# A banded attention and a gated feed-forward in one program: where the first weights stand in the load queue, and what the search for the order charges

## The chip, the cores and the metric

The kernel runs on one core of one Trainium2 chip. The metric is the device time of an execution in microseconds (us), median of three runs. A core has four engines that matter here, each with a queue of its own that is worked off in order: PE (matrix multiply into PSUM; its weight loads are shown apart as PEld), DVE (vector), ACT (scalar and activation), POOL. SP only starts transfers (DMA); they too start in the order of its queue.

## The reference

Attention for 4 batches, 8 heads, 768 positions, head size 64, in which a query sees the keys less than 96 positions behind it and the first 8 keys; a bias of -slope times distance is added ahead of the softmax. The heads of a position side by side are a row of 512 numbers, and each of the 3072 rows goes through a gated feed-forward (called "moe" in the code):

```
x = attention(q, k, v)              # [3072, 512]
out = ((x @ w_a) * (x @ w_b)) @ w_out   # w_a, w_b [512, 1536], w_out [1536, 512]
```

The inputs are float64 and reach the chip as pairs of 32-bit words.

## The kernel before

The 3072 rows are cut into 24 blocks of 128, and these into 8 units of 4, 2, 3, 3, 3, 3, 3 and 3 blocks (`UNITS`). For a unit the attention gives `x`; the feed-forward then runs over `NF` = 12 chunks `f` of 128 hidden columns. The attention of unit u+1 is worked in beside the feed-forward of unit u, so only the first unit's attention has no matrix work to hide behind.

**Attention of the first unit** (`first`, `quad`). It goes by four pairs of heads, c = 0 to 3, each in two halves j. For a half: scores `ps` on PE (line 789), the maximum on DVE (617), exp on ACT (633), sum and reciprocal on DVE (648, 655), normalizing on DVE, POOL or ACT (667, 665), transposes `pt` on PE (692), copies `pf` to SBUF (419), and the product with the values into `pa` on PE (742). After both halves of pair c, `pa` is written as two parts, `xh` (rounded for PE, line 419) and the rest `xl` (DVE, 849); for pair 3 the names of both tiles are `xl0` and `xl0_3`. The second unit is done in the same way with one half for a pair (`ps..1_c_0`). Inputs of pair c are `raw0_c` (queries and keys) and `v0_c`, loaded by `fetch_first` through SP (line 544). Pair 0's `raw0` is loaded and scaled ahead of that.

**Weights** (`load_w`). Chunk f comes in two pieces, g = 0 and 1, of 768 KB: `wr{f}_{g}` (line 455). Piece 0 holds the chunk of `w_a` and half of that of `w_b`, piece 1 the rest and `w_out`. Each is turned from float64 into a rounded and a rest part, `wt{f}_{g}`, by seven or eight steps of 768 columns: ACT 461 (absolute value of the high word) and 498 (low word); DVE 468, 478 (clip, shift), 488, 507 (join); the cast to the rounded part on ACT (419) or DVE (421); the rest on DVE (429). This is done once, beside the first unit, and the pieces stay.

**Feed-forward** (`moe`). For a chunk, `p0` and `p1` (line 990) take 12 matmuls each, three for each pair c: xh by the rounded weight, xl by it, xh by the rest. ACT copies `p0`, DVE multiplies by `p1` (1029), the result is split into `hh` and `hl` (419 or 421, 429), and line 1008 adds the product with `w_out` to the accumulators `acc`.

**What sets the order.** Every step is given to a planner (`Schedule.op`) with a due time `due` in ns, the engines that may do it and a cost on each. `Schedule.order` hands out the steps: an engine that is free takes, of the steps whose inputs are there, the one due first. What it writes is the order of each engine's queue; on the chip each step then waits for its inputs only. `Schedule.search` looks for better due times for all steps due ahead of `t2`, which is the end of the second unit's feed-forward: it shifts a share of the due times by random amounts and keeps a trial that ends earlier.

```
START = 52000
WLEAD = 6000
TRIES = 400
SHARE = 0.03
SPREAD = 4000.0
...
        loads = [self.fetch_first(c, -1e6 + 2 * c) for c in range(NCC)]
...
        for f in range(NF):
            self.load_w(f, t + f * steps[0] - WLEAD)
```

So in this plan the inputs of all four pairs are due ahead of everything, and the loads of chunk 0 are due at 46000 with their other steps; SP, which takes what is due first, starts the weights right after the seven inputs.

Of the kernel before, what the change touches and what calls it, by code (L numbers as in the profile page):

```python
# [27 lines left out]
NCC = DM // P  # L28
# [15 lines left out]
OLD = ()  # L44

START = 52000
WLEAD = 6000
LOADLEAD = 8000
SPLITLEAD = 3000
# [6 lines left out]
SWAP = 640.0  # L56
PRICE = {"dve": 2.0, "pool": 2.0}


TRIES = 400  # L60
SHARE = 0.03
SPREAD = 4000.0
TRACE = False
LAGS = {"pe": 200.0, "act": 270.0, "dve": 230.0, "pool": 290.0, "dma": 2300.0}
BIG = float(2**38)
# [149 lines left out]
class Schedule:  # L215
# [22 lines left out]
    def search(self, limit, tries, share, spread):  # L238


        rnd = random.Random(1)
        ops = [op for op in self.ops if op.due < limit]
        dues = {op.index: op.due for op in ops}
        best = self.order(ops, dues)[1]
        for _ in range(tries):
            trial = dict(dues)
            for op in ops:
                if rnd.random() < share:
                    trial[op.index] += rnd.gauss(0.0, spread)
            end = self.order(ops, trial)[1]  # L250
            if end < best:
                best, dues = end, trial
        return self.order(self.ops, {op.index: dues.get(op.index, op.due) for op in self.ops})

    def order(self, ops, dues):
        for op in ops:
            op.fresh(dues[op.index], dues)
        for op in ops:
            for buf in op.bufs:
                buf.left += 1  # L260
        free = {e: 0.0 for e in self.SYNC}
        ready = {e: [] for e in self.SYNC}
        heap = []
        head = {t: 0 for t in self.tags}
        live = {t: 0 for t in self.tags}
        taken = set()
        out = []
        now = 0.0
        port = 0.0

        def arrive(op):
            for e in op.costs:
                insort(ready[e], (op.at, op.index, op))

        def fits(op):
            for b in op.bufs:
                if b in taken:
                    continue
                queue = self.tags[b.tag]
                if head[b.tag] >= len(queue) or queue[head[b.tag]] is not b or live[b.tag] >= b.bufs:  # L280
                    return False
            return True

        def wins(op, e):
            if len(op.costs) == 1:
                return True
            at = {}
            for o, c in op.costs.items():
                at[o] = max(free[o], now) + c * PRICE.get(o, 1.0)
                for due, index, other in ready[o]:  # L290
                    if (due, index) >= (op.at, op.index):
                        break
                    if len(other.costs) == 1 and fits(other):
                        at[o] += BACKLOG * other.costs[o]
            return at[e] <= min(at.values()) + 40.0

        for op in ops:
            if not op.before:
                arrive(op)
        while len(out) < len(ops):  # L300
            started = True
            while started:
                started = False
                for e in free:
                    if free[e] > now:
                        continue
                    for item in ready[e]:
                        op = item[2]
                        if e in op.port and port > now:
                            continue  # L310
                        if fits(op) and wins(op, e):
                            break
                    else:
                        continue
                    for o in op.costs:
                        ready[o].remove(item)
                    for b in op.bufs:
                        if b not in taken:
                            taken.add(b)
                            head[b.tag] += 1  # L320
                            live[b.tag] += 1
                    op.engine = e
                    op.t0 = now
                    out.append(op)
                    free[e] = now + op.costs[e]
                    if e in op.port:
                        port = free[e]
                    heappush(heap, (free[e], 0, op.index, op))
                    started = True
            if not heap:  # L330
                raise RuntimeError("no order")
            now, kind, _, op = heappop(heap)
            if kind == 0:
                for nxt in op.after:
                    if nxt.index not in dues:
                        continue
                    if op.engine == "pe" and tuple(nxt.costs) == ("pe",):
                        lag = 0.0
                    else:
                        lag = (op.lag or self.SYNC[op.engine]) + nxt.spare  # L340
                    nxt.ready = max(nxt.ready, now + lag)
                    nxt.before -= 1
                    if not nxt.before:
                        heappush(heap, (nxt.ready, 1, nxt.index, nxt))
                heappush(heap, (now + (op.lag or self.SYNC[op.engine]), 2, op.index, op))
            elif kind == 1:
                arrive(op)
            else:
                for b in op.bufs:
                    b.left -= 1  # L350
                    if not b.left:
                        live[b.tag] -= 1
        return out, now


def act(n, psum=False):
# [18 lines left out]
class Fast:  # L375
# [61 lines left out]
    def load_w(self, f, due):  # L437
# [3 lines left out]
        for g in range(2):  # L441
# [9 lines left out]
            mi = lambda m0=m0: self.wm[:, m0 : m0 + WN]  # L451
            m = lambda mi=mi: mi().bitcast(F32)
            op(
                due,
                lambda e, f=f, g=g, raw=raw: nc.sync.dma_start(raw[:, :].bitcast(I64), self.wts[f, g]),
                writes=[(raw, "lo"), (raw, "hi")],
                dma=2184,
# [364 lines left out]
    def first(self, end):  # L822


        sp = self.sbuf
        six = [sp([P, 3 * WIDE], F32R, k, k + "0") for k in ("xh", "xl")]
        two = [sp([P, 512], F32R, "o", f"xl0_{c}", 2) for c in (2, 3)]
        xh = [(six[0], 0), (six[0], WIDE), (six[0], 2 * WIDE), (six[1], 0)]
        xl = [(six[1], WIDE), (six[1], 2 * WIDE), (two[0], 0), (two[1], 0)]
        homes = {  # L830
            "q": ("hl", WIDE),
            "s": (("psS", "acc0"), ("p0", "acc2")),
            "pt": ("psT", "p1", "acc1"),
            "t": (("kk", MAXK), ("raw", MAXC)),
            "pf": (("hh", WIDE), ("v", 2 * MAXV * D)),
        }
        loads = [self.fetch_first(c, -1e6 + 2 * c) for c in range(NCC)]
        step = end / NCC
        for c in range(NCC):
            pa = self.bank("psA", f"pa0_{c}")  # L840
            for j in range(2):
                self.quad(0, c, j, c * step + (j + 1) * step / 2, *loads[c], pa, homes)
            (hi, h0), (lo, l0) = xh[c], xl[c]
            get = lambda b, b0=0: lambda: b[:, b0 : b0 + WIDE]
            due = (c + 1) * step
            self.copy(due, get(hi, h0), get(pa), WIDE, [pa], [(hi, c)], psum=True)
            self.plan.op(
                due,
                lambda e, lo=get(lo, l0), hi=get(hi, h0), pa=get(pa): self.nc.vector.tensor_sub(
                    lo(), pa(), hi()  # L850
                ),
                [pa, (hi, c)],
                [(lo, -c - 1)],
                dve=dve(WIDE),
            )
        return xh, xl
# [211 lines left out]
    def run(self):  # L1068
        self.open()
        t = START  # L1070
        x = self.first(t - 3000)
        steps = []
        for u, pl in enumerate(PLANS):
            nxt = PLANS[u + 1].nb if u + 1 < len(PLANS) else 0
            steps.append(24 * pe(pl.nb * P) + pl.nb * 3 * pe(512) + nxt * H * 700 / NF)
        xs = {0: x}

        def ahead(u, t):
            xs[u] = self.attention(u, t, t + (NF - SLACK) * steps[u - 1])

        for f in range(NF):
            self.load_w(f, t + f * steps[0] - WLEAD)
        t2 = t + NF * (steps[0] + steps[1])
        for u in range(len(UNITS)):
            self.moe(u, t, steps[u], xs[u])
            if u + 1 < len(UNITS):
                ahead(u + 1, t)
            t += NF * steps[u]
        order, end = self.plan.search(t2, TRIES, SHARE, SPREAD)
        if TRACE:  # L1090
            print('MODEL', end)
        with self.tc.manual_schedule():
            for op in order:
                op.emit(op.engine)
# [371 lines left out]
```

## Time and profile before

| | |
|---|---|
| time, median of 3 runs | 741.05 us (739.51 to 741.62) |
| profiled execution | 739.72 us, of which its span of instructions 737.9 us |
| busy share of the span | PE 97%, PEld 87%, DVE 65%, ACT 47%, POOL 1% |
| granted PE clock, mean | 0.994 |
| chain that ended last, by engine | PE 92%, DVE 4%, ACT 2%, DMA 1% |
| transfers | 74.58 MB, mean 101 GB/s, over 300 GB/s in the first tenth of the span |

A row of the profile names line, engine, operation and tiles (output<-input) with shapes, `x` the count, then the time; a bracket gives the idle time of the engine just before and what ended it. A row of stretches gives, for each engine, busy us and in parentheses the count of instructions; then the clock that PE was granted (1.00 is full), the share of the transfer engines, and GB/s. PE's busy time has its clock in it: at half clock the same matmul is busy for twice as long.

### The profile page before, as it was taken

How to read it: one execution, taken by the hardware profiler on the slowest of the kernel's cores; microseconds unless marked ns; L12 is line 12 of the kernel's file. 1: busy time of each engine (PE TensorE's matmuls, PEld its weight loads, DVE VectorE, ACT ScalarE, POOL GpSimd, SP SyncE). 2: the span in 40 equal slices, each digit the busy share in tenths (PEclk: the TensorE clock that was granted, in tenths of full speed). 3: DMA queues.
4: the chain of work that ended last, by engine and by line, in shares of the span. 5: the costliest groups of instructions: out<-in, count | busy, mean ns of one | idle time of the engine just before them, and what ended most of it. 6: DMA issues, size and time to landing. Idle time of an engine off the chain costs nothing.

```text
span 737.9 us, 12581 instructions
## 1 busy us (share of the span) xinstructions
PE 715.4 (97%) x4344; PEld 640.1 (87%) x4344; DVE 480.0 (65%) x1574; ACT 348.8 (47%) x891; POOL 8.9 (1%) x28
## 2 busy tenths in 40 slices
PE   5789999999999999999999999999999999999996
PEld 4567877889988999999999999999999999899996
DVE  5999999958956776287744878268672876321111
ACT  6999967556335353254424544154432544331112
POOL 1000000000000000000000000000000000000000
PEclk9999999999999999999999999999999999999999
DMA  7898211123533234124231443214341242110001
GB/s 282 345 339 326 82 32 33 35 85 110 142 106 113 84 98 116 44 83 110 74 116 44 108 122 96 73 61 107 88 128 55 81 127 62 47 44 0 1 1 47
DMA packets 38520, 74.58 MB, mean 101 GB/s; under 512 B 8496, under 2 KB 21040, under 8 KB 38448
## 3 DMA queue, kind: packets, MB, share of 16 engines
q1 hardware_dynamic: 29232, 65.03, 27.6%
q10 hardware_dynamic: 9216, 8.66, 4.6%
q8 instruction: 36, 0.59, 0.3%
q14 instruction: 36, 0.29, 0.1%
HBM read 50.07 MB, written 6.29 MB: 76 GB/s over the span
## 4 chain that ended last, share of the span: by engine, by line
PE 92%; DVE 4%; ACT 2%; DMA 1%; issue 0%; DVEq 0%; ACTq 0%; SPq 0%
PE p L990 54%; PE acc L1008 27%; PE pa L742 5%; PE ps L915 4%; PE ps L789 2%; DVE t L617 1%; PE pt L692 1%; DMA v<-qkv 0%; DMA nv<-ns 0%; DMA raw<-qkv 0%; DVE kk L429 0%; DVE t L667 0%; ACT kk L419 0%; ACT xh L419 0%; ACT wr L498 0%
## 5 line engine op out<-in xcount | busy, mean ns | idle before, releaser
L990 PE MATMUL p<-xh,wt 128*128 128x384 f32 (+2 forms) x1488 | 418.3, 338 | 1.1 <-DVE wt L429 0.6
L990 PEld LDWEIGHTS p<-xh,wt 128*128 128x128 f32 x1488 | 270.3, 188 | 15.3 <-issue 3.4
L990 PE MATMUL p<-xl,wt 128*128 128x384 f32 (+2 forms) x816 | 270.1, 341 | 0.3 <-DVE xl L429 0.3
L1008 PE MATMUL acc<-wt,hh 128*128 128x512 f32 x576 | 202.5, 394 | 0.0
L990 PEld LDWEIGHTS p<-xl,wt 128*128 128x128 f32 x816 | 153.9, 189 | 10.1 <-issue 1.0
L1008 PEld LDWEIGHTS acc<-wt,hh 128*128 128x128 f32 x576 | 108.2, 188 | 20.5 <-issue 1.3
L1029 DVE TENSOR_TENSOR raw<-p,raw 128x384 f32<-128x384 f32 (+2 forms) x96 | 52.9, 551 | 96.6 <-PE p L990 93.1
L1008 PE MATMUL acc<-wt,hl 128*128 128x512 f32 x288 | 113.1, 393 | 0.0
L633 ACT ACTIVATE t<-t,sm 128x232 f32<-128x232 f32 (+2 forms) x120 | 56.5, 472 | 93.9 <-DMA pf<-wm 77.6
L419 ACT COPY raw<-p 128x384 f32<-128x384 f32 (+2 forms) x84 | 39.9, 475 | 104.1 <-PE p L990 101.5
L1008 PEld LDWEIGHTS acc<-wt,hl 128*128 128x128 f32 x288 | 54.2, 188 | 7.6
L429 DVE TENSOR_TENSOR hl<-raw,hh 128x384 fp32r<-128x384 f32 (+2 forms) x95 | 52.1, 548 | 12.7 <-ACT hh L419 12.0
L617 DVE CUSTOM_DVE_ANT_0 t<-ps,rel 128x232 f32<-128x232 f32 (+1 forms) x100 | 38.1, 397 | 25.6 <-PE ps L915 23.2
L419 ACT CAST hh<-raw 128x384 fp32r<-128x384 f32 (+2 forms) x69 | 35.5, 515 | 39.2 <-DVE raw L1029 33.0
L742 PEld LDWEIGHTS pa<-pf,v 128*64 128x64 f32 x640 | 35.5, 138 | 13.0 <-issue 7.4
L742 PE MATMUL pa<-pf,v 128*64 128x128 f32 x640 | 43.7, 280 | 2.9 <-ACT pf L419 1.3
L633 ACT ACTIVATE wm<-wm,sm 128x232 f32<-128x232 f32 (+2 forms) x72 | 34.0, 472 | 23.8 <-DVE sm L617 20.1
L429 DVE TENSOR_TENSOR kk<-raw,kk 64x348 fp32r<-64x348 f32 (+1 forms) x90 | 41.6, 463 | 2.8
L915 PE MATMUL ps<-kk,ql 128*128 128x232 f32 (+2 forms) x144 | 39.4, 275 | 0.0
L915 PE MATMUL ps<-kk,qh 128*128 128x232 f32 (+2 forms) x144 | 38.5, 270 | 0.5 <-DVE sm L617 0.4
L665 ACT ACTIVATE wm<-wm,sm 128x232 f32<-128x232 f32 (+2 forms) x58 | 27.5, 478 | 23.3 <-DVE sm L655 21.0
L709 DVE STREAM_TRANSPOSE wm<-wm 128x256 f32<-128x256 f32 (+1 forms) x72 | 29.6, 414 | 6.7 <-ACT wm L665 5.7
(87 smaller groups left out, 666.8 us busy)
## 6 DMA issues: line engine op xcount, KB each, us to landing
wr<-wts SPq DMA_DIRECT2D x24, 768.0 KB, 10.8
raw<-qkv SPq DMA_DIRECT2D x24, 366.0 KB, 3.1
raw<-qkv SPq DMA_DIRECT2D x24, 314.0 KB, 2.9
v<-qkv SPq DMA_DIRECT2D x16, 384.0 KB, 3.1
out<-o SPq DMA_DIRECT2D x23, 256.0 KB, 2.1
pf<-wm SPq DMA_DIRECT2D x96, 48.0 KB, 2.0
pf<-wm ACTq DMA_DIRECT2D x96, 48.0 KB, 2.0
v<-qkv SPq DMA_DIRECT2D x16, 256.0 KB, 2.7
```

The source lines that it names most:

```text
L419: self.nc.scalar.copy(out(), src())
L429: lambda e: self.engine(e).tensor_sub(out(), a(), b()),
L617: lambda e, j=j, o=o, w=w, neg=neg: nc.vector.tensor_tensor_reduce(t[:, o : o + w], ps[:, o : o + w], neg[:, :w], -(2.0 ** -(h + 1)), 3.0e ...
L633: lambda e, j=j, o=o, w=w: nc.scalar.activation(t[:, o : o + w], t[:, o : o + w], AF.Exp, bias=sm[:, j : j + 1], scale=-1.0, accum_out=sm[ ...
L665: nc.scalar.mul(t[:, o : o + w], t[:, o : o + w], r)
L709: nc.vector.transpose(dst, src)
L742: nc.tensor.matmul(pa[D * s : D * s + D, i * P : i * P + P], v[:, v0 : v0 + D], probs[s, i][1](c), start=c == 0, stop=c == len(slots) - 1,)
L789: nc.tensor.matmul(ps[s][:, o : o + w], qs[r, q0 + m * P : q0 + m * P + P], raw[r, kc : kc + w], start=True, stop=True,)
L915: nc.tensor.matmul(ps[:, :w], q[:, i * P : i * P + P], kk[:, k0 : k0 + w], start=m == 0, stop=m == 1,)
L990: nc.tensor.matmul(p[:, :T], wt(), b[:, b0 : b0 + T], start=c == 0 and n == 0, stop=c == NCC - 1 and n == 2,)
L1008: nc.tensor.matmul(acc[i][:, :], hs[:, i * P : i * P + P], wt(), start=f == 0 and n == 0, stop=f == NF - 1 and n == 2,)
L1029: lambda e, asb=asb, pb=pb: nc.vector.tensor_mul(asb[:, :T], pb[:, :T], asb[:, :T]),
```

## The change

Three things. The load of chunk 0's weights (not its other steps) gets a due time of its own, so that piece 0 is due between the inputs of pair 0 and pair 1, and piece 1 between those of pair 1 and pair 2; the inputs' own due times are spread to make room. The search counts, beside the end of the plan, a charge for waits of PE: for each step on PE the part of the wait ahead of it that exceeds 1300 ns is counted twice, up to 1300 ns a wait. And it makes 1200 trials instead of 400, each shifting 1% of the due times (3% before) by a spread of 8000 ns (4000 before).

```diff
+EARLY = -60000
+LOAD = 4000
...
+IDLE = 1300.0
+FINE = 2.0
...
-TRIES = 400
-SHARE = 0.03
-SPREAD = 4000.0
+TRIES = 1200
+SHARE = 0.01
+SPREAD = 8000.0
...
-        best = self.order(ops, dues)[1]
+        best = self.order(ops, dues)[1:]
...
-            end = self.order(ops, trial)[1]
-            if end < best:
-                best, dues = end, trial
+            found = self.order(ops, trial)[1:]
+            if sum(found) < sum(best):
+                best, dues = found, trial
...
+                    if e == "pe":
+                        fine += min(max(now - free[e] - IDLE, 0.0) * FINE, IDLE)
...
-                due,
+                EARLY + (2 * g + 1) * LOAD if f == 0 else due,
                 lambda e, f=f, g=g, raw=raw: nc.sync.dma_start(raw[:, :].bitcast(I64), self.wts[f, g]),
...
-        loads = [self.fetch_first(c, -1e6 + 2 * c) for c in range(NCC)]
+        loads = [self.fetch_first(c, EARLY + 2 * c * LOAD) for c in range(NCC)]
```

Nearly every row of PE, DVE and ACT up to the end of the second unit changes its place. Three places are shown. Line numbers are 9 higher in the changed kernel; `wr0_1` is chunk 0, piece 1; `raw0_2` and `v0_2` are pair 2 of the first unit; the number at the end of a name is only a count.

The queue of SP from the first load of the plan, before and then now:

```order
L544 DMA v0_0_149<-qkv 128x768
L544 DMA raw0_1_160<-qkv 128x1232
L544 DMA v0_1_178<-qkv 128x768
L544 DMA raw0_2_187<-qkv 128x1232
L544 DMA v0_2_219<-qkv 128x768
L544 DMA raw0_3_237<-qkv 128x1232
L544 DMA v0_3_267<-qkv 128x768
L455 DMA wr0_0_284<-wts 128x768
L455 DMA wr0_1_323<-wts 128x768
L455 DMA wr1_0_355<-wts 128x768
```

```order
L553 DMA v0_0_149<-qkv 128x768
L464 DMA wr0_0_160<-wts 128x768
L553 DMA raw0_1_181<-qkv 128x1232
L553 DMA v0_1_197<-qkv 128x768
L464 DMA wr0_1_211<-wts 128x768
L553 DMA raw0_2_245<-qkv 128x1232
L553 DMA v0_2_271<-qkv 128x768
L553 DMA raw0_3_287<-qkv 128x1232
L553 DMA v0_3_310<-qkv 128x768
L464 DMA wr1_0_326<-wts 128x768
```

Piece 0 moved ahead of six inputs, piece 1 ahead of four; what follows from chunk 1 on stands as it did.

The queue of ACT where it begins the second pair of heads (`t0_0_1_0` is the first half of pair 1), before and then now:

```order
L419 COPY pf1_0_0_0_211<-pt1_0_0_0_200 128x384
L665 ACTIVATE t1_0_0_1_175<-t1_0_0_1_175,sm1_0_0_1_176 128x232
L665 ACTIVATE t0_0_0_1_169<-t0_0_0_1_169,sm0_0_0_1_170 128x232
L633 ACTIVATE t0_0_1_0_234,sm0_0_1_0_235<-t0_0_1_0_234,sm0_0_1_0_235 128x128
L633 ACTIVATE t1_0_1_0_239,sm1_0_1_0_240<-t1_0_1_0_239,sm1_0_1_0_240 128x128
L633 ACTIVATE t0_0_1_0_234,sm0_0_1_0_235<-t0_0_1_0_234,sm0_0_1_0_235 128x256
L419 COPY pf0_0_0_1_265<-pt0_0_0_1_244 128x512
```

```order
L428 COPY pf1_0_0_0_209<-pt1_0_0_0_199 128x384
L470 ACTIVATE wm_219<-wr0_0_160 128x768
L674 ACTIVATE t1_0_0_1_173<-t1_0_0_1_173,sm1_0_0_1_174 128x232
L781 ACTIVATE qs0_1_1_233<-raw0_1_181,sc_79 128x256
L428 COPY pf0_0_0_1_242<-pt0_0_0_1_213 128x512
L507 ACTIVATE wr0_0_160<-wr0_0_160 128x768
L642 ACTIVATE t0_0_1_0_253,sm0_0_1_0_254<-t0_0_1_0_253,sm0_0_1_0_254 128x128
```

Both ACT steps of chunk 0's first piece (470, 507) now stand ahead of the second pair's exp; before, the first of them stood 19 rows further down, behind the second pair's exps.

The queue of PE at the end of the first unit's attention: `pa0_3` is the last product with the values, `ps0_1_0_0` the scores of the second unit's first pair, `p00_0` and `p10_0` chunk 0 (the rows with `xl0`, `xl0_3` are its last pair), `p00_1` chunk 1. Before and then now:

```order
L742 MATMUL pa0_3_564<-pf1_0_3_1_608,v0_3_267 64x128
L789 MATMUL ps0_1_0_0_644<-raw1_0_550,qs1_0_0_638 128x232
L789 MATMUL ps1_1_0_0_646<-raw1_0_550,qs1_0_0_638 128x232
...
L990 MATMUL p00_0_540<-xl0_332,wt0_0_525 128x512
L990 MATMUL p00_0_540<-xl0_3_640,wt0_0_525 128x512
...
L990 MATMUL p00_1_671<-xh0_321,wt1_0_635 128x512
```

```order
L751 MATMUL pa0_3_573<-pf1_0_3_1_603,v0_3_310 64x128
L999 MATMUL p10_0_596<-xh0_297,wt0_1_519 128x512
L999 MATMUL p10_0_596<-xl0_2_557,wt0_1_519 128x512
...
L798 MATMUL ps0_1_0_0_635<-raw1_0_569,qs1_0_0_630 128x232
L798 MATMUL ps1_1_0_0_637<-raw1_0_569,qs1_0_0_630 128x232
...
L999 MATMUL p00_0_483<-xl0_308,wt0_0_417 128x512
L999 MATMUL p00_0_483<-xl0_3_646,wt0_0_417 128x512
...
L999 MATMUL p00_1_665<-xh0_297,wt1_0_628 128x512
```

Three matmuls of chunk 0's third pair now stand between the last product with the values and the scores; `qs1_0_0`, on which the scores wait, was ACT's (row 75 of its queue, behind the last `xh` and a cast) and is now a DVE step ahead of the last `xl`.

More of the change, by code (lines that the diff above doesn't have):

```diff
@@ L269, in order @@
         port = 0.0
+        fine = 0.0
         def arrive(op):
@@ L352, in order @@
                         live[b.tag] -= 1
-        return out, now
+        return out, now, fine
 def act(n, psum=False):
@@ L1088, in run @@
             t += NF * steps[u]
-        order, end = self.plan.search(t2, TRIES, SHARE, SPREAD)
+        order, end, _ = self.plan.search(t2, TRIES, SHARE, SPREAD)
         if TRACE:
```

## The prediction

> **What bounds the kernel now.** I read the page first, then the busy time by stretches, then the timeline at the largest hole.
>
> ```profile
> span 737.9 us, 12581 instructions
> 12.30:24.00 11.70, 11.32 (x100) 8.34 (x97) 8.92 (x51) 10.44 (x36) 0.00 (x0) 0.85 1.02 418
> 24.00:43.30 19.30, 15.85 (x131) 11.17 (x128) 18.76 (x64) 19.30 (x50) 0.74 (x2) 1.00 0.83 320
> 43.30:46.30 3.00, 0.05 (x3) 0.03 (x2) 3.00 (x5) 3.00 (x6) 0.00 (x0) 1.00 0.74 227
> 49.80:60.00 10.20, 10.20 (x45) 8.04 (x44) 9.40 (x19) 10.20 (x20) 0.00 (x0) 1.00 0.99 401
> 60.00:97.00 37.00, 37.00 (x194) 29.24 (x192) 36.72 (x70) 33.43 (x57) 0.00 (x0) 1.00 0.41 157
> 97.00:145.00 48.00, 48.00 (x244) 37.86 (x243) 47.41 (x89) 31.54 (x62) 2.01 (x2) 1.00 0.10 26
> 160.00:205.00 45.00, 44.71 (x353) 41.32 (x354) 40.53 (x177) 23.98 (x81) 0.71 (x1) 1.00 0.45 128
> 205.00:230.00 25.00, 23.81 (x169) 21.22 (x166) 16.62 (x64) 13.76 (x37) 2.02 (x2) 1.00 0.39 112
> 230.00:700.00 470.00, 469.26 (x2850) 434.93 (x2849) 276.88 (x966) 181.83 (x499) 1.42 (x2) 1.00 0.28 80
> ```
>
> Columns: stretch, length, then busy us of PE, PEld, DVE, ACT and POOL, PE's clock, the transfers. From 49.8 us to the end PE hardly stops (470 us with 0.74 idle between 230 and 700). The edit removes no matrix work, so it can only win where PE stands or runs slowly: before 50 us, and in the 1.48 us of idle between 160 and 230 (0.29 + 1.19). Before 43 us PE waits because ACT (19.30 of 19.30) and DVE (18.76) are full. Both had time to spare earlier: 1.26 us of ACT and 2.78 of DVE between 12.3 and 24. The hole itself:
>
> ```profile
> 41.12 1.06 ACT L419 COPY pf<-pt 128x512 f32<-128x512 f32 x2
> 41.75 1.57 PE L742 MATMUL pa<-pf,v 128*64 128x128 f32 x16
> 42.06 1.77 ACT L498 ACTIVATE wr<-wr 128x768 int32<-128x768 uint32 x2
> 43.69 0.91 ACT L461 ACTIVATE wm<-wr 128x768 f32<-128x768 f32 x1
> 44.48 0.59 ACT L419 CAST xl<-pa 128x512 fp32r<-128x512 f32 x1
> 45.37 0.68 DVE L849 TENSOR_TENSOR xl<-pa,xl 128x512 fp32r<-128x512 f32 x1
> 45.67 0.54 ACT L772 ACTIVATE qs<-raw,sc 128x256 f32<-128x256 f32 x1
> 46.27 1.79 PE L789 MATMUL ps<-raw,qs 64*128 64x232 f32 x8 [2.95 <-ACT qs L772]
> 48.05 7.42 PE p L990 x27
> 80.39 3.50 PE p L990 x15
> L461 ACT ACTIVATE wm<-wr 128x768 f32<-128x768 f32 x8 | 7.3, 916 | 0.0
> L498 ACT ACTIVATE wr<-wr 128x768 int32<-128x768 uint32 x12 | 10.7, 925 | 0.0
> ```
>
> The last product with the values ends at 43.32. ACT has three weight steps to do before it writes the last `xh` at 44.48; DVE then writes the last `xl`, ready at 46.05; and PE, at the head of its queue, waits 2.95 us for `qs`, computes scores, and starts chunk 0's last pair only at 48.05, though the inputs were there 2 us earlier. The three rows below the hole give prices: 3.50 us for 15 matmuls at full clock, 0.233 each, and the two weight steps of ACT.
>
> **PE's clock there.** By stretches of 3.41 us:
>
> ```profile
> 8.90:12.31 3.41, 1.48 (x12) 0.98 (x13) 3.41 (x22) 3.21 (x13) 0.00 (x0) 1.00 1.01 401
> 12.31:15.72 3.41, 3.41 (x25) 2.43 (x22) 2.54 (x15) 2.38 (x9) 0.00 (x0) 0.50 1.01 407
> 29.37:32.79 3.42, 2.15 (x18) 1.35 (x13) 3.42 (x19) 3.42 (x12) 0.37 (x1) 1.00 0.98 402
> 43.03:46.44 3.41, 0.46 (x6) 0.22 (x5) 3.41 (x6) 3.41 (x6) 0.00 (x0) 1.00 0.79 255
> 46.44:49.85 3.41, 3.41 (x12) 2.39 (x13) 2.60 (x6) 2.39 (x4) 0.00 (x0) 0.50 1.01 360
> ```
>
> Each of the two stretches at half clock follows one with little work (1.48 and 0.46 us busy); after one with 2.15 the clock stayed. So a hole costs its length and up to 1.7 us (half of 3.41) behind it. The Trainium skill, "TensorE: Matmul & The Clock Gate", Part 1, says that the clock halves after an idle window of some 3.4 us, and that the windows run free. Taken literally (an idle window) this would not have dropped the clock at 12.31, so the trace is stricter than the page; by the page the new hole below is harmless, by the trace it is so only under about 1.3 us (3.42 - 2.15); the sum is the same by both.
>
> **The change, part by part.**
>
> *The loads.*
>
> ```profile
> 5.80 0.33 SPq L544 DMA_DIRECT2D v<-qkv  x1
> 6.18 0.43 SPq L544 DMA_DIRECT2D raw<-qkv  x1
> 9.05 10.62 SPq L455 DMA_DIRECT2D wr<-wts  x9
> 11.43 0.35 DVE L774 TENSOR_SCALAR qs<-raw,sc 128x256 f32<-128x256 f32 x1
> wr<-wts SPq DMA_DIRECT2D x24, 768.0 KB, 10.8
> ```
>
> No transfer is added; two of 0.79 MB move ahead. At the 401 GB/s of the row from 8.90 that is 2.0 us each. Pair 1's input then lands 2.0 us later, pairs 2 and 3 3.9 us later, piece 0 six places earlier. Counting from 7.5 us (0.39 + 0.79 + 0.63 MB), `raw0_1` is there at about 12.0. DVE reaches its first step on it (11.43 before) behind four more short softmax steps, at about 12.3: bounds of the wait 0 and, if the queued transfers share the engines instead of following each other, 3 us. I take 0. The later pairs are needed after 19 us and land before that.
>
> *ACT and DVE up to the last `xl`.* Adding the steps of each queue by their durations, DVE has 0.06 us more to do up to that point than before, ACT 0.27 up to the last `xh` (one more weight cast and a `qs` instead of a low-word step and a copy). What can come earlier is only the spare time: the two weight steps of ACT (0.92 us each) and four of DVE now stand in it. ACT can win 1.26 - 0.27 = 1.0 us at most, and nothing if pair 1's later scores (they stand behind pair 0's first product with the values) open new waits as long. I take 0.5: last `xh` at 44.0, `xl` ready at 45.5.
>
> *PE at the hole.* The last product with the values ends at about 42.8 (ACT's three weight steps again stand between). Then three matmuls of chunk 0 (3 x 0.233 = 0.70), and the scores, 0.9 us at full clock, as `qs` is DVE's and stands 1.35 us of steps ahead of `xl`. They fill the hole to 44.6; 0.9 us remain, which keep the clock. Chunk 0's last pair starts at 45.5 instead of 48.05: **-2.55 us** (-3.05 to -2.05 by the bounds above). From 48.05 to 49.85 PE ran at half clock: **-0.9 us** more. Lead at 50 us: 3.45 us.
>
> *What DVE takes back.* PE may keep the lead only where the weights are ready.
>
> ```profile
> 95.34 0.95 DVE L429 TENSOR_TENSOR wt<-wm,wt 128x768 fp32r<-128x768 f32 x1
> 97.00 0.39 PE L990 MATMUL p<-xh,wt 128*128 128x512 f32 x1
> 101.89 0.95 DVE L429 TENSOR_TENSOR wt<-wm,wt 128x768 fp32r<-128x768 f32 x1
> 107.69 0.63 PE L990 MATMUL p<-xh,wt 128*128 128x512 f32 x2
> L419 ACT CAST wt<-wm 128x768 fp32r<-128x768 f32 x3 | 2.5, 841 | 0.0
> L421 DVE CAST wt<-wm 128x768 fp32r<-128x768 f32 x3 | 1.7, 555 | 0.0
> ```
>
> Chunk 6 is the narrow place: its first piece is ready at 96.29, and PE uses the rest part with its third matmul at 97.46, 1.2 us later. DVE was idle for 0.80 + 0.28 us from 49.8 to 97, and 0.75 in the 46.44 row. The new queue has 1.15 us more of DVE steps ahead of this point (two casts that were ACT's, a product that stood behind). So a lead of 1.2 + 0.5 + 1.83 - 1.15 = 2.4 us at most can pass, and 0.6 if DVE recovers none of its idle time. As PE runs ahead, the products that DVE waits for come earlier too, so most is recovered, and I take 2.1, near the upper end: **+1.35 us**. For chunk 7 the same step ends at 102.84 and is used at 107.69, 4.9 us later; DVE's further 1.3 us of moved casts fit into that.
>
> *The second unit.* The next unit's scores now come closer together at its start, where DVE has room (97 to 145: 47.41 of 48, but from 160 on 40.53 of 45). This may close part of the 1.48 us of idle, or, with the swap transfers between, lose as much; the row of before does not show it. Bounds -1.48 and +1.5, I take **-0.3**.
>
> Sum: -2.55 - 0.9 + 1.35 - 0.3 = -2.4, so 737.3 us against this execution's own 739.72 (737.9 of span, 1.8 around it). It was 1.33 us quicker than the median of the runs, 741.05. The changed kernel's starts will differ from run to run too, as holes before 16 us remain; I add half, 0.6, for its median: **737.9 us**.
>
> **Rivals.** Faster or slower means by over 0.3% of 741.05 (2.2 us), about what runs of this kernel can tell apart: below 738.8, above 743.3.
>
> - *DVE takes the whole lead back.* It is full from 24 to 145 us in either order, and the search does not shorten its work. Then only the 0.6 of the bound above and the second unit's -0.3 remain: 739.72 - 0.9 + 0.6 = 739.4, no change. For: 36.72 of 37.00. Against: 1.83 us of idle time between 46 and 97.
> - *The early weights hold up pair 1* (the other side). SP's queue gives 0.79 MB ahead of `raw0_1`; if the transfers share the engines, DVE stands in order at `qs`, with the weight steps behind it, for 3 us, and at pair 2 for about as long again. A stand of 3.5 us cancels the lead; 6 us make the hole at 43 us longer and bring the half clock back: 739.7 + 2.5 + 0.9 = 743.1, with the run's offset 743.7. For: 10.8 us median from issue to landing, much of it behind others. Against: `raw` landed before 11.43, ahead of all that was queued behind it.
> - *The clock drops again.* If ACT comes 0.5 us later than I take it, the hole passes 1.3 us; half clock takes up to 1.7 back: 739.6. For: the fixed order of three ACT weight steps ahead of the last `xh`.
> - *All comes through*: DVE gives back 0.6 us only and the second unit closes 1.2 us of its idle time: 739.72 - 2.85 - 1.2 + 0.6 = 736.3, or 735.3 with ACT's full 1.0.
> - *Nothing happens*: excluded; the queues differ from the first rows on.
>
> **Chances.** Forecast 0.48, between 736.8 and 738.9; whole lead taken back 0.22; clock again 0.08; all through 0.14; pair 1 held up 0.08. Of the forecast nearly all, and all of the fourth rival, are below 738.8: faster 0.58, within 0.3% 0.34, slower 0.08. The range leaves out the worst of the held-up case and the best of the fourth: 735.3 to 740.8.
>
> **What would show it.**
>
> ```profile
> 23.66 0.89 ACT L461 ACTIVATE wm<-wr 128x768 f32<-128x768 f32 x1
> ```
>
> In the trace after: ACT's first weight step near 13 us instead of 23.66; no wait of PE over 1.3 us between 16 and 50, and full clock from 45 to 50; the first matmul with the last `xl` near 45.5; chunk 6 starting 2 us earlier than 97.00, with short waits of PE for `wt` ahead of it; the unit of 256 columns with less than 1.5 us of idle. I am wrong if DVE stands long at the first `qs` of pair 1, if PE waits repeatedly for `wt` or `hl` between 55 and 97, or if the second unit's swap transfers leave PE idle by more than 3 us.

## The result, and the profile after

The changed kernel takes 735.66 us (median of 6 runs, 735.14 to 737.54) against 741.51 for the kernel before (6 runs): a ratio of 0.9930, 95% interval 0.9914 to 0.9946. The profiled execution took 735.88 us, of which 734.0 are span. The forecast was 737.9, with 735.3 to 740.8 as its range: the direction and the mechanism at the hole held, but the gain is 5.9 us where 3.2 were forecast, and 2.4 us of it come from a term that the sum had at 0.3. The measured time lies 0.4 us above the lower end of the range.

The stretches of the prediction, from the trace of the changed kernel (columns as there):

```profile
core 0 of [0], span 734.0 us
...
12.30:24.00 11.70, 9.97 (x79) 6.89 (x80) 9.74 (x44) 10.81 (x31) 0.37 (x1) 1.00 1.02 419
24.00:43.30 19.30, 16.77 (x152) 12.13 (x148) 18.81 (x73) 19.30 (x57) 0.74 (x1) 1.00 0.77 299
43.30:46.30 3.00, 2.79 (x14) 1.74 (x15) 3.00 (x6) 3.00 (x5) 0.00 (x0) 1.00 0.97 343
49.80:60.00 10.20, 10.20 (x46) 8.22 (x45) 10.00 (x23) 10.20 (x21) 0.00 (x0) 1.00 1.01 418
60.00:97.00 37.00, 37.00 (x197) 28.96 (x196) 36.82 (x70) 31.47 (x54) 0.00 (x0) 1.00 0.42 158
97.00:145.00 48.00, 48.00 (x241) 38.16 (x240) 47.51 (x93) 30.08 (x59) 1.76 (x2) 1.00 0.10 26
160.00:205.00 45.00, 44.69 (x355) 41.16 (x354) 40.60 (x176) 23.81 (x80) 3.00 (x4) 1.00 0.46 131
205.00:230.00 25.00, 24.32 (x163) 22.68 (x162) 14.57 (x47) 9.04 (x23) 0.00 (x0) 1.00 0.32 94
230.00:700.00 470.00, 468.89 (x2850) 434.68 (x2849) 279.05 (x980) 183.40 (x505) 1.42 (x2) 1.00 0.28 80
```

The hole is gone: PE works 2.79 of the 3.00 us from 43.3 on (0.05 before). DVE is as full as it was from 24 to 145 us, and ACT in the rows up to 60 us; behind that ACT has a little less to do (31.47 us of 37 where it had 33.43). From 205 to 230 PE idles 0.68 us instead of 1.19. The timeline at the former hole, with ACT's first weight step ahead of it:

```profile
12.94 0.91 ACT L470 ACTIVATE wm<-wr 128x768 f32<-128x768 f32 x1
...
44.11 1.05 PE L798 MATMUL ps<-raw,qs 64*128 64x232 f32 x8
44.38 0.63 ACT L428 CAST xl<-pa 128x512 fp32r<-128x512 f32 x1
...
44.85 2.55 ACT L507 ACTIVATE wr<-wr 128x768 int32<-128x768 uint32 x3
45.06 0.68 DVE L858 TENSOR_TENSOR xl<-pa,xl 128x512 fp32r<-128x512 f32 x1
...
45.80 1.43 PE L999 MATMUL p<-xl,wt 128*128 128x512 f32 x5 [0.21 <-DVE xl L858]
...
47.27 0.60 ACT L428 COPY raw<-p 128x512 f32<-128x512 f32 x1
...
47.92 0.50 PE L999 MATMUL p<-xh,wt 128*128 128x512 f32 x1 [0.69 <-ACT raw L428]
```

The first matmul with the last `xl` starts at 45.80 instead of 48.05, the scores take 1.05 us instead of 1.79, and the clock is full. Then comes a wait that the prediction did not have: ACT does three weight steps in a row (44.85 to 47.40) before it copies chunk 0's `p`, and PE stands for 0.69 us.

To say where time was won I use the *lead*: every form of matmul counts with its median interval in the trace of before, and the lead of another trace is how much earlier it has done the same sum of matmul work. It is a derived figure; two pairs of rows bear it out, from the timeline and from the group of line 990 (999 after), whose second time is the start of the last such matmul. Before:

```profile
154.46 0.28 PE L990 MATMUL p<-xh,wt 128*128 128x256 f32 x1
```

```profile
L990 PE MATMUL p<-xh,wt x1488: 276/335/504, 34.3 to 727.5; 128*128 128x384 f32 x144, 128*128 128x256 f32 x24, 128*128 128x512 f32 x18
```

After:

```profile
152.06 0.28 PE L999 MATMUL p<-xh,wt 128*128 128x256 f32 x1
```

```profile
L999 PE MATMUL p<-xh,wt x1488: 276/335/504, 31.8 to 723.4; 128*128 128x384 f32 x144, 128*128 128x256 f32 x24, 128*128 128x512 f32 x18
```

The second unit's feed-forward starts 2.4 us earlier, the last `p` 4.1 us. In between the lead is 2.4 us at 60 us, 2.4 still at 145, 4.8 at 250, and 4.1 at the end. So there are two gains, one at the hole and one in 190 to 245 us, and a small loss behind.

### The profile page after: what moved, and what is told of

Same layout as the page of the kernel before. It is cut to its first block, busy times and chain, and to the rows that moved or that the text cites. A ratio compares the mean times of both kernels' runs of the same rounds, so it can differ in the third digit from the quotient of the medians.

```text
span 734.0 us, 12602 instructions
## 1 busy us (share of the span) xinstructions
PE 713.0 (97%) x4344; PEld 638.9 (87%) x4344; DVE 482.6 (66%) x1583; ACT 343.4 (47%) x881; POOL 9.3 (1%) x29
## 4 chain that ended last, share of the span: by engine, by line
PE 85%; DVE 5%; ACT 3%; DMA 3%; issue 1%; ACTq 1%; SPq 0%; DVEq 0%
PE p L999 50%; PE acc L1017 25%; PE pa L751 5%; PE ps L924 4%; DMA pf<-wm 2%; ACT t L642 1%; PE ps L798 1%; DVE wm L718 1%; PE pt L701 1%; ACTq L732 1%; DVE t L626 1%; ACT t L674 1%; DMA nv<-ns 0%; ACT wm L642 0%; DMA raw<-qkv 0%
## 5 line engine op out<-in xcount | busy, mean ns | idle before, releaser
L924 PE MATMUL ps<-kk,ql 128*128 128x128 f32 (+1 forms) x144 | 39.5, 275 | 0.0
L924 PE MATMUL ps<-kk,qh 128*128 128x128 f32 (+1 forms) x144 | 38.3, 268 | 0.0
L657 DVE TENSOR_SCALAR sm<-sm 128x1 f32<-128x1 f32 (+1 forms) x168 | 24.0, 146 | 16.9 <-ACT t L642 13.2
```

The costliest lines, as they stand in the source:

```text
L657: lambda e: nc.vector.tensor_scalar_add(sm[:, 2 * n : 3 * n], sm[:, n : 2 * n], 1e-9),
L924: nc.tensor.matmul(ps[:, :w], q[:, i * P : i * P + P], kk[:, k0 : k0 + w], start=m == 0, stop=m == 1,)
```

## The experiments

All twelve runs. Lead is that of the profiled execution of each over the trace of before shown above, at 60 us, at 250 us and at the last `p`. Ratios, with 95% intervals, are over all runs against those of the kernel before on the same chip (medians 741.77 to 741.98 there); they need not be the quotients of the two medians. The trace of before is some 2 us shorter than these medians, so a gain in the median comes out larger than a lead at the end.

| run | median us | ratio | profiled us | lead 60 / 250 / end |
|---|---|---|---|---|
| before again | 741.94 | 1.0002 (0.9993 to 1.0012) | 741.69 | -1.2 / -2.0 / -1.7 |
| after again | 735.49 | 0.9918 (0.9905 to 0.9930) | 735.27 | 2.7 / 5.3 / 4.3 |
| loads only | 737.11 | 0.9942 (0.9927 to 0.9957) | 738.03 | 2.4 / 2.0 / 1.7 |
| search only | 737.16 | 0.9946 (0.9930 to 0.9962) | 735.99 | 1.3 / 3.2 / 4.0 |
| no charge | 735.99 | 0.9925 (0.9911 to 0.9939) | 734.63 | 2.1 / 4.3 / 5.2 |
| charge, old tries | 740.99 | 0.9992 (0.9977 to 1.0007) | 739.19 | 1.1 / 0.3 / 0.3 |
| first unit new | 737.46 | 0.9940 (0.9928 to 0.9953) | 737.55 | 1.7 / 2.1 / 2.6 |
| later steps new | 738.84 | 0.9965 (0.9951 to 0.9979) | 738.42 | -0.1 / 1.2 / 1.2 |
| before, hole filled | 740.72 | 0.9986 (0.9975 to 0.9996) | 740.73 | 1.2 / 0.6 / -1.1 |
| after, hole again | 737.08 | 0.9932 (0.9919 to 0.9945) | 737.08 | 0.7 / 3.4 / 2.9 |
| warm start | 734.85 | 0.9905 (0.9890 to 0.9919) | 735.15 | 4.8 / 6.7 / 4.6 |
| warm start kept | 736.01 | 0.9911 (0.9892 to 0.9930) | 736.54 | 4.5 / 7.7 / 3.5 |

The theories: A, there are two gains, the hole (with the clock behind it) and the second unit's order; B, the early loads are the only lever; C, the charge is the lever.

**Both kernels once more.** No edit.

> The kernel before, unchanged, for a second trace of it. Its median in 11 runs was 741.98 us, and the trace shown was of a run of 739.72. Theory A (the runs differ by the moment at which TensorE's clock first rises, 8.9 us in the trace shown, and by what the free-running 3.41 us windows then meet): a run near 742 shows the first full clock later than 8.9 us, 12 to 17, or one half-clock stretch more in the first 50 us, and the 2 us are lost ahead of 50 us. Rival: the 2 us are lost in small steps in 160 to 700 us, with the clock as it was in the trace shown.

> The changed kernel unchanged, for a second trace and for a median on the chip on which the warm start is run again. Theory A: 735.4 to 736.2; full clock from 46 us on in this trace too, and the moment of the first full clock somewhere between 9 and 17 us. Rival (the first trace was a lucky phase of the windows): a half-clock stretch in 43 to 53 us.

The run of before took 741.69 us, and lost its 2.0 us against the trace shown in two places. The first is the clock (stretches of 3.41 us on the grid of this run):

```profile
42.28:45.69 3.41, 1.08 (x14) 0.83 (x14) 3.41 (x6) 3.41 (x6) 0.00 (x0) 1.00 0.74 232
45.69:49.10 3.41, 2.75 (x10) 1.99 (x11) 3.41 (x7) 3.05 (x5) 0.00 (x0) 0.50 0.97 396
49.10:52.52 3.42, 3.42 (x9) 2.63 (x9) 1.37 (x3) 2.41 (x6) 0.00 (x0) 0.50 0.92 327
```

Two stretches at half clock follow the hole, not one: the first of them has the rest of the hole in it (2.75 us busy) and the clock did not come back behind it. The second stretch costs 1.2 us of lead. The other loss, 0.75 us near 214 us, is a wait for ACT:

```profile
PE p L990 <- ACT raw L419: 1.1, 2, 0.8
```

So the trace that the prediction was made from was a lucky one: of the 51 runs of the kernel before that stood beside the experiments none was as short as its 739.72 us (739.83 to 743.29, their medians 741.77 to 741.98); of the six beside the result one was (739.51). The guess that a late first full clock does it was wrong: in this run it came at 14.97 us, 6 us later than in the trace shown, and the lead at 20 us was 0.00.

The changed kernel again (735.27) has full clock from 15.80 us on; neither of its two traces has a hole or a half-clock stretch at 43 to 53 us.

**The hole and the clock.** In the kernel before, the hole is filled with work that moves nothing forward:

```diff
+            for _ in range(24 * (u == 1 and c == 0)):
+                nc.tensor.transpose(ps[0][:, :P], self.ident, self.ident)
```

> The kernel before with 24 transposes of the identity, whose result nobody reads, ahead of the scores of the second unit's first pair: they fill TensorE's hole of 2.95 us at 43.3 us with work that moves nothing forward. Theory A (the half clock at 46.4 to 49.9 us follows from the hole): no half-clock stretch there, 0.9 us from the scores at 46.3 and 0.9 from the chunk behind them, 1.5 to 2 us less than before, 740 to 740.5. Rival (idle time alone costs, the clock drops whatever is done): within 0.5 us of before. If the dummies run beyond the moment at which the scores could start: slower by up to 1 us.

```profile
41.89:45.31 3.42, 3.38 (x36) 3.06 (x35) 3.42 (x6) 3.42 (x6) 0.00 (x0) 1.00 0.60 187
45.31:48.72 3.41, 3.17 (x20) 2.12 (x18) 3.41 (x8) 3.41 (x6) 0.00 (x0) 1.00 1.01 408
```

No half clock is left, and the lead at 60 us is 1.2 us, with the hole's length unchanged: that is what the clock behind the hole costs when one stretch is halved, and 2.5 us against the run with two. The median gains 1.2 us (741.88 to 740.72), a little less than theory A's 1.5 to 2. The profiled execution gave its lead away later, in waits of PE of 0.8 to 1.0 us at 212, 541 and 661 us. The clock's part of the first gain is thus shown; the idle part is the other 1.2 us of the 2.4, a remainder that no run shows by itself.

The reverse was less clean. In the changed kernel the scores and their `qs` go behind the last `xl`:

```diff
+        for op in self.moved:
+            order.remove(op)
+        at = order.index(self.last) + 1
+        order[at:at] = self.moved
```

> The changed kernel with the scores of the second unit's first pair (and the split of their q) moved behind the last xl of chunk 0, so that TensorE again has a hole ahead of them near 44 us. Theory A (a hole of this size makes the clock drop for one or two windows of 3.41 us, each worth 0.9 to 1.2 us where TensorE is the bound): 1.3 us of idle and 1 to 2.5 of half clock, 738 to 739.5, with a half-clock stretch between 45 and 53 us. Rival (only the idle time counts): 736.5 to 737.3 and full clock.

```profile
34.47:37.88 3.41, 1.78 (x20) 1.30 (x21) 3.41 (x15) 3.41 (x13) 0.00 (x0) 1.00 0.08 34
37.88:41.29 3.41, 3.41 (x18) 2.33 (x18) 2.67 (x9) 3.15 (x7) 0.00 (x0) 0.50 0.47 135
44.71:48.12 3.41, 2.15 (x14) 1.35 (x13) 2.83 (x6) 3.41 (x6) 0.00 (x0) 1.00 0.79 258
48.12:51.54 3.42, 3.42 (x14) 2.48 (x15) 2.81 (x5) 2.79 (x6) 0.00 (x0) 1.00 0.96 349
```

The hole came back with 1.26 us, and the clock stayed full behind it: theory A's half-clock stretch at 45 to 53 us is refuted for a hole of this size, since 2.15 us of work were left in its stretch. It cost 1.6 us in the median (735.49 to 737.08). In this trace another stretch fell to half clock, at 37.88 behind one with 1.78 us of work; the 2.0 us that the trace is behind at 60 us hold both, so the price of the 1.26 us alone stays open. The rival (only idle time counts: 736.5 to 737.3 and full clock) came nearer than theory A.

**Which part of the change.** Loads only: the new due times in the kernel before.

```diff
-        loads = [self.fetch_first(c, -1e6 + 2 * c) for c in range(NCC)]
+        loads = [self.fetch_first(c, EARLY + 2 * c * LOAD) for c in range(NCC)]
...
-                due,
+                EARLY + (2 * g + 1) * LOAD if f == 0 else due,
```

> The kernel before with the new due times of chunk 0's weight loads alone; the search stays as it was (400 trials, the end as its only measure, no charge). Theory A (the hole at 43 to 46 us and the half clock behind it are worth 2.4 us, and the loads are what moves them): the first matmul with the last xl starts near 45.5 to 46.5 us, no half-clock stretch at 46 to 50, and 2 to 3 us less than before, 738.0 to 739.5; the second unit (160 to 230 us) keeps its old time. Rival B (the loads are the only lever): all of the change's 5.9 us, 735 to 736. Rival C (the charge in the search is the lever): within 1 us of before.

Search only: these two edits undone in the changed kernel.

> The changed kernel with chunk 0's weight loads due where they were before; the search keeps its charge and its 1200 trials. Theory A: the hole before 46 us is shortened only if the search finds work for it with late loads; if it doesn't, what is left is the gain of the second unit, 2 to 2.5 us, and the time is 738.5 to 739.5. Rival B (the loads are the only lever): within 1 us of before. Rival C (the charge is the lever): all of the 5.9 us, 735 to 736, with the hole gone.

No charge: `FINE = 0.0` in the changed kernel.

> The changed kernel with the charge on waits of TensorE set to zero; early loads and 1200 finer trials stay. Theory A: which order the search ends in is partly chance, but the loads fill the hole as long as the weights are first: 736 to 738.5, the second unit's part (2.4 us) in doubt. Rival B: 735 to 736.5, as after. Rival C: no better than 740.

Charge with old tries: `TRIES = 400`, `SHARE = 0.03`, `SPREAD = 4000.0` in the changed kernel.

> The changed kernel with the old 400 trials of the search (each moves 3% of the steps by 4 us) in place of 1200 (1% by 8 us); early loads and the charge stay. Theory A (the loads give 2.4 us at 46 us, the second unit's 2.2 us come from the longer search): as the loads alone, 737 to 738, with the lead over the kernel before 2.4 us up to 200 us and no more than 2.5 behind 240. Rival C (the charge finds the second unit's order): as the changed kernel, 735.5 to 736, with a lead above 4 us behind 240.

Loads alone give 4.9 us in the median and the whole first gain (lead 2.4 at 60 us, as with all of the change) and nothing in the second unit (2.0 at 250). The search alone gives 4.8 us in the other way: 1.3 at 60 us, and 1.9 more by 250. Both are better than theory A had them (738.0 and 738.5 at best), and the two overlap: together they give 6.3 us, not 9.7. The intervals of the loads alone and of the whole change overlap, so what the search adds to the loads is shown by the traces and not by the medians. With the loads where they were the search shortened the hole, but not enough for the clock:

```profile
42.22:45.64 3.42, 1.63 (x20) 1.38 (x22) 3.42 (x6) 3.42 (x7) 0.00 (x0) 1.00 0.86 283
45.64:49.05 3.41, 3.41 (x12) 2.34 (x9) 3.12 (x6) 3.20 (x5) 0.00 (x0) 0.50 0.79 261
```

B falls, as the search with late loads gains as much; C falls too. Without the charge the gain is the same (735.99, interval of the ratio 0.9911 to 0.9939, beside 0.9905 to 0.9930 with it). With the charge and the old trials hardly anything is left, though the loads are early: 740.99, 3.9 us above the loads alone, where theory A had 737 to 738 and C 735.5 to 736. That order has a lead of only 1.1 us at 60 us, and two long waits in the second unit ("issue" is a wait that nothing in the profile ended):

```profile
PE pa L751 <- DMA pf<-wm: 1.6, 1, 1.6
PE pa L751 <- issue: 1.3, 1, 1.3
```

```profile
215.15:218.56 3.41, 2.00 (x15) 1.52 (x13) 2.07 (x6) 1.57 (x4) 0.00 (x0) 1.00 0.32 84
```

In the profiled execution (739.19) the clock stayed full behind 2.00 us of work; over its 12 runs the five with a mean clock of 0.993 or less took 741.05 to 743.87, the seven others 738.13 to 741.95. That other runs fall to half clock there fits, and is not shown, as only one of them has a trace. So of the search it is not the charge but the longer and finer trying that goes with the second gain: the three orders that it found have it (2.4, 1.9 and 2.2 us of lead between 60 and 250 us, with the loads late, too), and of the orders by the old trials neither the loads alone (-0.4) nor the one with the charge (-0.8) does. Number, share and spread of the trials were put back together, so which of them counts is open. Each edit also sends the random trials another way; one order for each setting doesn't tell how much of a difference is that.

**Where in the program.** The due times found with and without the change are mixed: steps due before the end of the first unit's feed-forward from the one, the later ones from the other.

```diff
+        new = self.plan.search(t2, TRIES, SHARE, SPREAD)
...
+        old = self.plan.search(t2, 400, 0.03, 4000.0, False)
+        dues = {op.index: (FIRST if op.due < t1 else SECOND)(new, old)[op.index] for op in ops}
```

> The order of the first unit's steps (all steps due before the end of its feed-forward) from the changed kernel, the order of all later steps as found before. Theory A (two gains in two places): 2.4 us at 46 us come through, the 2.4 us of the second unit don't, so 2 to 3.5 us less than before, 738 to 739.5, with the lead over the kernel before constant from 48 us on. Rival B (everything is in the first unit): as after, 735 to 736. Rival C (the lead of the first unit is handed back where later steps were planned for the old start): within 1 us of before.

> The order of the first unit's steps and chunk 0's loads as before, the order of all later steps from the changed kernel. Theory A (two gains in two places, which add): no gain up to 160 us, 2 to 2.5 us in 160 to 230 us, so 739 to 740. Rival B (all in the first unit): within 1 us of before. Rival D (the second unit's order gains only where it starts early): within 1 us of before too, with the waits of 160 to 230 us as before.

New first steps give 4.5 us, new later steps 3.0 us, each a little more than theory A had (738 and 739 at best); the sum, 7.5, is near the 6.3 of both together, so the gains add, roughly. With the later steps alone the start is that of before, hole and half clock included,

```profile
43.27:46.68 3.41, 0.45 (x6) 0.23 (x4) 3.41 (x6) 3.41 (x6) 0.00 (x0) 1.00 0.77 256
46.68:50.09 3.41, 3.41 (x13) 2.38 (x12) 2.53 (x6) 2.39 (x4) 0.00 (x0) 0.50 0.95 354
```

and the lead goes from -0.1 at 60 us to 1.2 at 250, though it is -1.4 at 199 us in between. Rival D is refuted: the second unit's order gains without an early start. (The trace shows 1.3 us of the 3.0 of the median; it has one halved stretch behind the hole, like the trace of before shown above, and the typical run of before may have two.)

**A version that goes on from there.** In both traces of the changed kernel the first scores run at half clock. Warm start: ten matmuls of a constant tile at PE's start, while it waits for the first loads.

```diff
+                for _ in range(10):
+                    nc.tensor.matmul(junk, cold, cold, start=True, stop=True)
```

> The changed kernel with ten 128x128 matmuls of a constant tile ahead of all other work of TensorE, while it waits for the first loads; nobody reads their result. Theory A (the clock rises some microseconds after TensorE starts to work, and the first scores and rotations run at half clock until then, up to 16.6 us in the trace of the changed kernel): the clock rises earlier, before 12 us, the first scores take 1.6 us in place of 3.2, and the end comes 0.5 to 2 us earlier, 733.5 to 735.5. Rival (the first 40 us are set by DVE and ACT, 18.8 and 19.3 us busy of 19.3 between 24 and 43 us): the scores are faster, the end stays within 0.5 us of 735.7.

The same stretch of the changed kernel and then of the warm start:

```profile
5.60:8.90 3.30, 3.13 (x16) 2.46 (x16) 1.56 (x11) 1.55 (x6) 0.00 (x0) 1.00 0.53 184
```

```profile
5.60:8.90 3.30, 1.71 (x16) 1.38 (x16) 2.55 (x20) 2.42 (x10) 0.00 (x0) 1.00 0.63 207
```

Waits of the warm start, with total, count and longest:

```profile
PE pa L751 <- DMA pf<-wm: 2.4, 2, 1.2
...
PE p L999 <- ACT raw L428: 2.1, 2, 1.5
```

(In the first row of stretches the clock column says 1.00 only because its record begins later, at 16.57 us; the 16 scores took 3.13 us.) The clock is full from 5.16 us on, the scores take half the time, and the lead at 60 us is 4.8 us, 2.1 to 2.4 more than in the two traces of the change alone. Of the 6.7 us at 250 us the profiled execution lost 2.1 up to the end, above all in a wait of 1.2 us for the turned probabilities `pf` at 534 us and one of 1.5 for ACT's copy of `p` at 655. The median, 734.85 against 735.49, is within theory A's range and the best of all kernels, but not separated from the change: the intervals of the ratios overlap.

Warm start kept: 14 transposes more ahead of the first rotations.

```diff
+            for _ in range(14 * first):
+                nc.tensor.transpose(pt[:, :P], self.ident, self.ident)
```

> The changed kernel with ten matmuls of a constant tile at TensorE's start, and 14 transposes of the identity ahead of the first rotations, where TensorE waits 1 to 2 us for the softmax of the first pair; nobody reads the results. Theory A (run to run the clock still drops after the short busy stretch at 9 to 12 us: the runs with the warm start alone show mean clocks of 0.995 to 0.999): the mean clock is 0.998 or more in every run, 734 to 735 with less spread than the 733.95 to 736.15 of the warm start alone. Rival (the fillers hold up the rotations, or DVE and ACT set that stretch): no better than the warm start alone, 734.5 to 735.5.

Full clock from 5.24 us on and a lead of 7.7 us at 250, more than any other; then

```profile
PE pa L755 <- DMA pf<-wm: 2.2, 1, 2.2
```

```profile
428.50:431.91 3.41, 1.24 (x14) 0.80 (x15) 1.65 (x7) 2.44 (x8) 0.00 (x0) 1.00 0.41 112
431.91:435.32 3.41, 3.41 (x24) 3.08 (x21) 1.41 (x5) 0.94 (x3) 0.00 (x0) 0.50 0.17 27
```

a late transfer (3.3 us from issue to landing, where the median of these transfers is 2.0), and a half-clock stretch behind it. As the rival had it, the median is no better than that of the warm start. The expectation of a mean clock of 0.998 or more in every run was wrong (0.993 to 0.999); the fastest run, 732.38, is the one at 0.999, the rest lie between 734.73 and 736.88. What makes these transfers late in some runs and not in others is open.

## Why the prediction was right, and where not

The sum against the profiled execution, term by term; the measured leads are those of the trace of after (2.4 at 60 us and at 145, 4.8 at 250, 4.1 at the end).

| term | forecast us | measured us |
|---|---|---|
| hole and half clock | -3.45 | -2.4 |
| DVE takes back | +1.35 | 0 |
| second unit | -0.3 | -2.4 |
| behind 250 us | 0 | +0.7 |
| ends of the span | 0 | +0.2 |
| offset to the median | +0.6 | -0.2 |
| sum, from 739.72 | 737.9 | 735.7 |

- *The hole*: right in kind. ACT's first weight step stands at 12.94 (forecast 13), the last pair starts at 45.80 (45.5, from 48.05), the scores fill the gap, the clock holds. The step that "ACT wins 0.5 us" was mis-sized: its last cast for pair 3 starts at 44.38 against 44.48, 0.1 us earlier. And the sum ended at the start of the pair; the 0.69 us that PE then waits for ACT's copy of `p` was not in it. The later start (0.3 us) and this wait (0.7) are nearly the 1.05 us that are missing. A queue that is filled with moved steps up to a point is full behind that point too.
- *What DVE takes back*: wrong as a mechanism. I limited the lead at chunk 6 to 2.1 us, with DVE's rest part as the narrow place. The trace:

```profile
94.73 1.82 DVE L438 TENSOR_TENSOR wt<-wm,wt 128x768 fp32r<-128x768 f32 x2
95.37 1.05 PE L798 MATMUL ps<-raw,qs 64*128 64x232 f32 x8
96.35 0.50 PE L999 MATMUL p<-xh,wt 128*128 128x512 f32 x1
```

  In the new order the scores of the second unit's third pair stand ahead of chunk 6, so the chunk starts only 0.65 us earlier than before (96.35 for 97.00), when its weights are there, while PE did other work that had to be done anyway: eight scores and three products with `w_out` more than before up to this point, 1.6 us by their medians. The lead by work stayed 2.4 us from 60 to 145 us without a wait of PE. A limit on one chunk's start is no limit on the lead where the order gives PE something else to do. The forecast sign "chunk 6 two us earlier, with short waits of PE for `wt`" failed with it. That this term and the hole's together (2.1 us) come near the 2.4 measured is luck: a smaller lead came in than the sum had, and nothing held it back.
- *The second unit*: mis-sized by eight times, the largest error of the sum. I took the idle time, 1.48 us, as the most that could come, and 0.3 of it. The lead grew by 2.4 (2.6 in the second trace of after). Idle time of PE in 205 to 230 us fell by 0.5 only (23.81 to 24.32 busy). Nearly half of the rest lies in matmuls that took longer while PE counted as busy: between 200 and 250 us the intervals from one `p` to the next exceed the medians of their forms by 1.2 us in sum before (0.3 of it is idle time already counted), and by 0.2 at most after. What made them longer is not shown. "Busy" was read as "at full pace" though weight loads stood at 21.22 of 25 us there and at 22.68 after.
- *Against the runs*: half of the known offset was added for the median. The profiled execution of before was 2.2 us under the median of the later runs, with one half-clock stretch less behind the hole and one wait less than the run traced again; that of after was 0.2 above its own. The chance of a second half-clock stretch behind a hole is a cost of the hole, and belonged into its term.
- The four errors on the size of terms, +1.05, -1.35, -2.1 and +0.9, and -0.8 on the offset add to -2.3 us; the result is 2.2 under the forecast. Errors of both signs cancelled in part, so that the time fell inside the range owes something to luck.
- *Rivals*: that DVE takes the whole lead, that pair 1 is held up, and that the clock drops again: none of them came in the two traces of the change. Pair 1's `raw` landed at 12.7 us (forecast 12.0, before 10.4), ahead of DVE's first step on it at 13.37, and neither DVE nor ACT waited for an input between 9.2 and 24 us. PE is behind at the start all the same, by 2.5 us at 25 us; by 43 us it is 0.6. The loads alone show this too (2.0 us at 20 us), the search alone doesn't (0.2). "All comes through" (736.3) is nearest in time, by way of the second unit.
- *The clock rule*: the prediction put the bound between 1.48 and 2.15 us of work in a stretch of 3.41. Fourteen traces narrow it. Highest that was followed by half clock, from the run without the charge, and lowest that was not, from the warm start:

```profile
9.53:12.95 3.42, 1.95 (x12) 1.18 (x13) 3.07 (x19) 3.25 (x13) 0.00 (x0) 1.00 0.98 395
```

```profile
15.40:18.81 3.41, 1.95 (x21) 1.37 (x19) 3.41 (x17) 3.41 (x15) 0.37 (x1) 1.00 1.01 410
```

  Up to 700 us all thirteen full-clock stretches with 0.46 to 1.95 us of work were followed by half clock, and none of those with 1.95 or more other than the row shown first. The Trainium skill, "TensorE: Matmul & The Clock Gate", Part 1, puts the drop behind an idle window and says that the windows are free-running. The free grid agrees (first full clock at 8.9 to 17.2 us in the twelve traces without the warm start); the idle window doesn't: a stretch that is a little over half busy drops the clock.

## What to carry to other kernels

Price a hole on the critical engine as its length plus the clock behind it: here one halved stretch cost 1.2 us, in one of three traces with the hole a second followed, and filling the hole with useless work was already worth 1.2 us. Bound a gain by the pace of the work (equal work done at equal times) and not by idle time, and take a limit on one step for a limit on the whole only where nothing else can be put ahead of it. A random search's result is one draw: change one setting at a time and look at each order for its waits, as 400 trials with the charge lost what the moved loads alone had won.

## What the runs showed of the hardware

- In these traces TensorE's clock went by the share of work in stretches of 3.41 us on a grid that differs from run to run: half clock followed under 1.95 us of work (57%), full clock returned behind the thirteen half-clock stretches that were 3.41 us busy, and did not behind the one with 2.75. The same kernel had one or two halved stretches behind the same hole of 3.0 us, as the grid falls.
- Run-to-run spread may be partly this, though no trace shows it: a kernel with a wait near that bound in its second unit varied by 5.7 us over 12 runs (738.13 to 743.87), the changed kernel by 2.4 over 11 (735.14 to 737.54).
- Between 400 and 700 us PE waited 0.9 to 2.2 us at a time for turned probabilities or for ACT's copy behind them in three profiled executions (hole filled, and both warm starts), and 0.6 at most in the eleven others. Two of the three were further ahead than any other. On the chain that led to the wait for the turned probabilities, one transfer took 5.1 us (hole filled), 5.3 (warm start) and 3.3 (warm start kept) from issue to landing, where the median is 2.0 in every trace; why is open.
